# Attention over packed tokens and a Mish layer: both first batches' attention ahead of block 2, a fixed order on all engines up to block 15, and a d_ff order that alternates between batches 0 and 1

## Chip, core and metric

The kernel runs on 1 core of one Trainium2 chip. The metric is device time in microseconds (us) of one execution; lower is better. Float32 arithmetic is carried out on TensorE (PE) as sums of products of float32r halves, so that one product costs three matmuls.

## Reference

For 8 batches of 8 heads, 576 tokens and head width 64, 32 packed tokens per head attend to all keys, and then all queries attend to the packed result. The outcome, 4608 rows of 512, goes through a layer of width 2048 with the Mish function:

```python
p_packed = sm_attn(p, k, v)               # per head: 32 x 64
out = sm_attn(q, p_packed, p_packed)      # per head: 576 x 64
x = out.transpose(0, 2, 1, 3).reshape(B * S, H * D)
h = x @ w_in                              # 4608 x 2048
g = h * tanh(log1p(exp(min(h, 20))))      # Mish; h itself above 20
return g @ w_out                          # 4608 x 512
```

q, k, v and p are float32. The two weight matrices arrive as float64, and the kernel itself turns their 32-bit words into float32.

## The kernel before

**Attention of a batch** (class `Batch`). Eight heads are handled as two groups g of four. `load` issues the DMAs of k, p, q and v. `start` transposes p. `score(g)` transposes the keys (12 PE transposes, three evacuations, tile `kT`), multiplies with p, takes the maxima and subtracts them (L181); `exps` takes the exponentials on ScalarE (ACT) and their sums on VectorE (DVE, L191). `turn(g)` transposes the queries, `turn_weights` the exponentials, `values` multiplies them with v, `turn_values` transposes the result into `ppT`. `match(g)` multiplies queries with `ppT`, and DVE transposes the scores in 32x32 squares (L240). `weigh` is the second softmax (maxima L248, subtraction L249, Exp L252, sums L254, reciprocal, product L257), a DVE transpose (L262) into `at`, and the split into `aT_hi` (ACT, L263) and `aT_lo` (DVE, L264).

**The layer.** Since the second attention only mixes 32 packed rows per head, `packed_w(b, c)` first multiplies `ppT` with 512 columns (chunk c, four chunks) of w_in (tiles `wi`, matmuls L338) and splits the result into `wp_hi` and `wp_lo` (L349, L350). A *block* is 128 columns f of d_ff for one batch. Its `up` is twelve matmuls of 288 columns (L388), six for each half hf, then Mish on ACT (L391, L393) into `g`; `halves` splits g into `g_hi` (L400) and `g_lo` (L401) on DVE. Its `down` is twelve matmuls of 512 columns (L405 to L407), three for each of four row chunks c, summed over the 16 blocks of a batch in four PSUM accumulators `acc`. The last 64 rows of two batches are done together every four blocks (`split`, `down_rest`).

**Weights.** One conversion takes 128 x 512 weights (0.5 MB of words, tile `w_st`): two ACT passes (L295, L296), then on DVE a clamp (L297), a shift (L298), a sign merge (L299) and the addition of the low word (L302). For w_out a split follows, `wo_hi` on ACT (L312) and `wo_lo` on DVE (L313). There are 32 conversions: 16 of w_in, four for each chunk, and 16 of w_out, one for each f. Converted w_in is written to DRAM and fetched again for later batches (`fetch_wi`).

**What sets the order.** PE runs in the order of the source. The other engines' order is chosen by the scheduler of the tile framework when the program is built, and all DMAs are issued on the queue of SyncE (SP). After the attention of batch 0 the loop over t = 0 to 129 begins: block t (batch t div 16, f = t mod 16) goes up while block t - 2 (`LAG`) goes down. During the blocks of batch b the attention of batch b + 1 is taken in small steps from a generator, three for each block. In the blocks of batch 0, two conversions are called for each block (L517), so that all 32 are called by block 11. The PSUM pools are `ps_acc` (4 buffers), `ps_h` (2, for up) and `ps_a` (2, for attention and `packed_w`).

Of the kernel before, what the change touches and what calls it, by code (L numbers as in the profile page):

```python
# [18 lines left out]
KVB = 7  # L19
W2K = 5  # L20
# [8 lines left out]
def body(  # L29
# [76 lines left out]
    def evacuate(dst, src, n=None):  # L106
        if n is None:
            nc.any.tensor_copy(out=dst, in_=src)
        elif n % 2:
            nc.scalar.copy(out=dst, in_=src)  # L110
        else:
            nc.vector.tensor_copy(out=dst, in_=src)

    def transposed(pool, src, g, dst):
        for i in range(NI):
            ps = psum(pool, [P, 4, R], "ps_kq")
            for h in range(4):
                nc.tensor.transpose(out=ps[:, h, :], in_=of_slot(src, g, h)[:, i, :], identity=ident[:R, :R])  # L118
            evacuate(dst[:, i, :, :], ps, i if pool is ps_acc else None)
            yield  # L120
# [15 lines left out]
    class Batch:  # L136
# [5 lines left out]
        def load(self):  # L142
            b = self.b
            self.k_t = [load_heads(k, b, g, "k_t") for g in range(2)]
            self.p_t = att.tile([P, 2, 2, D], F32, name="p_t", bufs=1)
            p_src = p[b].rearrange("(g h) n d -> (h n) g d", g=2)
            for u in range(2):
                nc.sync.dma_start(out=self.p_t[:, :, u, :], in_=p_src)
            self.q_t = [load_heads(q, b, g, "q_t") for g in range(2)]
            self.v_t = [load_heads(v, b, g, "v_t") for g in range(2)]  # L150

        def start(self, pool):
# [5 lines left out]
            self.a1 = att.tile([P, 2, 2, NI, R], F32, name="a1", tag="a", bufs=1)  # L158
# [27 lines left out]

        def exps(self, gs):
# [3 lines left out]
            nc.vector.reduce_sum(out=self.rs[:, gs], in_=a, axis=AX.X)  # L191
            nc.vector.tensor_scalar(out=self.rs[:, gs], in0=self.rs[:, gs], scalar1=1e-9, scalar2=None, op0=ALU.add)
            nc.vector.reciprocal(out=self.rs[:, gs], in_=self.rs[:, gs])

        def turn_weights(self, g, pool):
            self.a1T[g] = att.tile([R, 2, NI, P], F32, name="a1T")
            for u in range(2):
# [3 lines left out]
                evacuate(self.a1T[g][:, u], ps)  # L201
# [41 lines left out]
        def weigh(self, gs):  # L243
            n = gs.stop - gs.start
            G = n * (S // NP)
            a2 = self.a2[:, gs].rearrange("a h g n -> a (h g) n")
            mx = stat.tile([P, 2 * (S // NP)], F32, name="mx2")[:, :G]
# [4 lines left out]
            nc.scalar.activation(out=a2, in_=a2, func=AF.Exp, scale=scale)  # L252
            sm = stat.tile([P, 2 * (S // NP)], F32, name="sm2")[:, :G]
# [14 lines left out]
        def attention(self):  # L268
# [15 lines left out]
            for g in range(2):  # L284
                yield from self.match(g, ps_a)
            self.weigh(slice(0, 2))

    def from_double(dst, src):


        x = src.rearrange("p (n t) -> p n t", t=2)
        low, high = x[:, :, 0], x[:, :, 1]
        bits = dst.bitcast(I32)
        r = wts.tile([P, dst.shape[1]], I32, name="wround", tag="w2k", bufs=W2K)
        nc.scalar.activation(out=dst, in_=high.bitcast(F32), func=AF.Copy, scale=F64_SCALE)  # L295
        nc.scalar.activation(out=r, in_=low.bitcast(U32), func=AF.Copy, scale=2.0 ** -29)  # L296
        nc.vector.tensor_scalar(out=dst, in0=dst, scalar1=F64_HIGH, scalar2=-F64_HIGH, op0=ALU.min, op1=ALU.max)  # L297
        nc.vector.tensor_scalar(out=bits, in0=bits, scalar1=3, scalar2=None, op0=ALU.logical_shift_left)  # L298
        nc.vector.scalar_tensor_tensor(  # L299
            out=bits, in0=high, scalar=-0x80000000, in1=bits, op0=ALU.bitwise_and, op1=ALU.bitwise_or  # L300
        )
        nc.vector.tensor_tensor(out=bits, in0=bits, in1=r, op=ALU.add)  # L302

    def staged(src):
        st = wts.tile([P, 2 * DO], I32, name="w_st", tag="wstage", bufs=3)
        nc.sync.dma_start(out=st, in_=src)
        return st

    def load_wo(i):
        w = wts.tile([P, DO], F32, name="wo32", tag="w2k", bufs=W2K)  # L310
        from_double(w, staged(w_out_v[:, i, :]))
        nc.scalar.copy(out=wo_hi[i], in_=w)  # L312
        nc.vector.tensor_tensor(out=wo_lo[i], in0=w, in1=wo_hi[i].bitcast(F32), op=ALU.subtract)  # L313
# [3 lines left out]
    def load_wi(c, m):  # L317

        g = m // 2
        if m % 2 == 0:  # L320
            wis[0, c, g] = wts.tile([P, 2, FC], F32, name="wi", tag="w32", bufs=4)
        from_double(wis[0, c, g][:, m % 2], staged(w_in_v[:, m, c * 2 * FC:(c + 1) * 2 * FC]))
        if m % 2:
            nc.sync.dma_start(out=w_in_f32[c][:, g], in_=wis[0, c, g])

    def fetch_wi(b, c):
        for g in range(2):
            wis[b, c, g] = wts.tile([P, 2, FC], F32, name="wi", tag="w32", bufs=4)
# [243 lines left out]
```

## Time and profile before

| what | value |
|---|---|
| median of 3 runs | 822.78 us (821.28 to 823.4) |
| profiled execution | 822.64 us |
| its span, first to last instruction | 820.9 us |
| mean granted PE clock | 0.952 |
| PE busy | 768.2 us (94%) |
| DVE busy | 420.6 us (51%) |
| ACT busy | 336.0 us (41%) |
| DMA | 90.02 MB, mean 110 GB/s |

The span is 1.7 us shorter than the profiled execution's time. In the rows below, times are in microseconds from the span's start. A row of the timeline gives start, duration, engine, source line, operation, output and inputs, shapes and, in brackets, the idle time before it and what ended that. A row of groups gives the count, then busy time and mean nanoseconds of one, then idle time before. A row of a table by stretch gives the stretch, its length, then for PE, PE weight loads, DVE, ACT and GpSimd the busy time and the number of instructions, then the granted PE clock, the DMA share and GB/s.

### The profile page before, as it was taken

The page shows a single profiled execution, that of the slowest core. Times are in us where ns is not written, and L with a number is a line of the kernel's source. Part 1 is how long each engine was busy: PE and PEld are TensorE (multiplying, and loading weights), DVE is VectorE, ACT ScalarE, POOL GpSimd, SP SyncE. Part 2 cuts the span into 40 slices and gives each one's busy share as a digit, 9 for nine tenths or more (in the row PEclk, how much of TensorE's full clock was granted, in tenths as well). Part 3 has the DMA queues.
Part 4 walks back from the last instruction along what each step waited for, and adds up shares of the span by engine and source line. Part 5 has one row for each costly group of instructions (what it writes and reads, how often), then busy time and mean ns, then how long its engine had stood idle before and what let it go on. Part 6 is the DMA issues. An engine that isn't in the chain of part 4 may idle for free.

```text
span 820.9 us, 13745 instructions
## 1 busy us (share of the span) xinstructions
PE 768.2 (94%) x5584; PEld 610.4 (74%) x5584; DVE 420.6 (51%) x812; ACT 336.0 (41%) x766; POOL 0.7 (0%) x6
## 2 busy tenths in 40 slices
PE   6607789999999999999999999999999999999997
PEld 4406667787788787877778787877778787888886
DVE  4799895744373435544373435544373445533332
ACT  3557583435242353235242353335242353332221
POOL 0000000000000000000000000000000000000000
PEclk6557789999999999999999999999999999999999
DMA  9967673144311533144411433144311421131002
GB/s 256 287 226 231 207 243 95 52 139 138 110 52 52 143 95 111 52 138 139 110 52 52 132 107 111 52 137 140 110 52 52 122 67 53 52 103 52 1 1 64
DMA packets 43966, 90.02 MB, mean 110 GB/s; under 512 B 8576, under 2 KB 27008, under 8 KB 43904
## 3 DMA queue, kind: packets, MB, share of 16 engines
q1 hardware_dynamic: 43904, 89.15, 35.8%
q8 instruction: 44, 0.72, 0.4%
q14 instruction: 18, 0.15, 0.1%
HBM read 75.50 MB, written 13.63 MB: 109 GB/s over the span
## 4 chain that ended last, share of the span: by engine, by line
PE 88%; DMA 5%; DVE 4%; issue 1%; ACT 1%; SPq 0%; ACTq 0%
PE ps_h L388 25%; PE acc L405 16%; PE acc L407 14%; PE acc L406 14%; PE ps_kq L118 4%; DMA w_st<-in_moe_w_in_dram 4%; PE ps_w L338 4%; PE ps_s L127 3%; PE ps_rest L405 2%; PE ps_rest L407 2%; PE ps_rest L406 2%; PE ps_pp L209 1%; PE ps_a L200 1%; DMA k_t<-in_k_dram 1%; DMA w_st<-in_moe_w_out_dram 1%
## 5 line engine op out<-in xcount | busy, mean ns | idle before, releaser
L405 PE MATMUL acc<-wo_hi,g_hi 128*128 128x512 f32 x512 | 216.5, 423 | 0.0
L391 ACT ACTIVATE g<-ps_h 128x288 f32<-128x288 f32 (+1 forms) x256 | 98.5, 385 | 286.5 <-PE ps_h L388 250.5
L407 PE MATMUL acc<-wo_hi,g_lo 128*128 128x512 f32 x512 | 203.4, 397 | 0.0
L406 PE MATMUL acc<-wo_lo,g_hi 128*128 128x512 f32 x512 | 203.3, 397 | 0.0
L388 PE MATMUL ps_h<-aT_hi,wp_hi 128*128 128x288 f32 x512 | 159.3, 311 | 21.8 <-ACT aT_hi L263 21.1
L400 DVE CAST g_hi<-g 128x512 fp32r<-128x512 f32 x128 | 54.5, 426 | 239.7 <-ACT g L391 239.7
L388 PE MATMUL ps_h<-aT_lo,wp_hi 128*128 128x288 f32 x512 | 153.2, 299 | 1.9 <-DVE aT_lo L264 1.9
L388 PE MATMUL ps_h<-aT_hi,wp_lo 128*128 128x288 f32 x512 | 153.3, 299 | 0.0
L405 PEld LDWEIGHTS acc<-wo_hi,g_hi 128*128 128x128 f32 x512 | 97.4, 190 | 42.7 <-issue 20.4
L388 PEld LDWEIGHTS ps_h<-aT_hi,wp_hi 128*128 128x128 f32 x512 | 98.1, 192 | 39.6 <-ACT aT_hi L263 23.2
L407 PEld LDWEIGHTS acc<-wo_hi,g_lo 128*128 128x128 f32 x512 | 96.9, 189 | 23.7 <-DVE g_lo L401 0.2
L388 PEld LDWEIGHTS ps_h<-aT_lo,wp_hi 128*128 128x128 f32 x512 | 98.4, 192 | 11.3 <-DVE aT_lo L264 2.5
L406 PEld LDWEIGHTS acc<-wo_lo,g_hi 128*128 128x128 f32 x512 | 97.6, 191 | 8.6
L388 PEld LDWEIGHTS ps_h<-aT_hi,wp_lo 128*128 128x128 f32 x512 | 98.4, 192 | 0.0
L401 DVE TENSOR_TENSOR g_lo<-g,g_hi 128x512 fp32r<-128x512 f32 x128 | 88.2, 689 | 5.9
L350 DVE TENSOR_TENSOR wp_lo<-ps_w,wp_hi 128x512 fp32r<-128x512 f32 x64 | 41.3, 682 | 19.0 <-ACT wp_hi L349 19.0
L349 ACT CAST wp_hi<-ps_w 128x512 fp32r<-128x512 f32 x64 | 34.3, 588 | 32.8 <-PE ps_w L338 32.8
L338 PE MATMUL ps_w<-wi,ppT 64*32 64x512 f32 x512 | 35.7, 615 | 0.0
L118 PE MATMUL ps_kq<-ident,k_t 96*128 96x96 f32 x192 | 27.0, 273 | 9.0 <-issue 4.9
L118 PEld LDWEIGHTS ps_kq<-ident,k_t 96*128 96x128 f32 x192 | 23.1, 158 | 16.4 <-issue 6.4
L118 PE MATMUL ps_kq<-ident,q_t 96*128 96x96 f32 x192 | 26.6, 267 | 6.5 <-issue 2.9
L118 PEld LDWEIGHTS ps_kq<-ident,q_t 96*128 96x128 f32 x192 | 22.6, 154 | 13.1 <-issue 4.6
(81 smaller groups left out, 727.0 us busy)
## 6 DMA issues: line engine op xcount, KB each, us to landing
wi<-w_in_f SPq DMA_DIRECT2D x56, 512.0 KB, 4.5
k_t<-in_k_dram SPq DMA_DIRECT2D x32, 288.0 KB, 3.6
q_t<-in_q_dram SPq DMA_DIRECT2D x32, 288.0 KB, 4.8
v_t<-in_v_dram SPq DMA_DIRECT2D x32, 288.0 KB, 3.6
w_st<-in_moe_w_in_dram SPq DMA_DIRECT2D x16, 512.0 KB, 5.2
w_st<-in_moe_w_out_dram SPq DMA_DIRECT2D x16, 512.0 KB, 4.3
out_dram<-o SPq DMA_DIRECT2D x24, 192.0 KB, 2.5
w_in_f<-wi SPq DMA_DIRECT2D x8, 512.0 KB, 5.0
```

The lines of the kernel that those rows point to most:

```text
L118: nc.tensor.transpose(out=ps[:, h, :], in_=of_slot(src, g, h)[:, i, :], identity=ident[:R, :R])
L127: nc.tensor.matmul(out=ps[u][h * NP:(h + 1) * NP, :], lhsT=packT[u * D:(u + 1) * D, h * NP:(h + 1) * NP], rhs=xT[u * D:(u + 1) * D, :, h, ...
L338: nc.tensor.matmul(out=ps[g][h * NP:(h + 1) * NP, :], lhsT=ppTb[row:row + D, g, h * NP:(h + 1) * NP], rhs=wis[b, c, g][row:row + D, h // 2 ...
L349: nc.scalar.copy(out=hi, in_=ps[g])
L350: nc.vector.tensor_tensor(out=lo, in0=ps[g], in1=hi.bitcast(F32), op=ALU.subtract)
L388: nc.tensor.matmul(out=ps, lhsT=w[:, fs], rhs=a[:, g, cs], start=(n == 0), stop=(n == 5))
L391: nc.scalar.activation(out=self.act[:, hf * HALF:hf * HALF + m], in_=ps[:, :m], func=AF.Mish)
L400: nc.vector.tensor_copy(out=hi, in_=self.act)
L401: nc.vector.tensor_tensor(out=lo, in0=self.act, in1=hi.bitcast(F32), op=ALU.subtract)
L405: nc.tensor.matmul(out=acc, lhsT=hi[:, cs], rhs=wh, start=start, stop=False)
L406: nc.tensor.matmul(out=acc, lhsT=hi[:, cs], rhs=wl, start=False, stop=False)
L407: nc.tensor.matmul(out=acc, lhsT=lo[:, cs], rhs=wh, start=False, stop=stop)
```

## The change

1. **Order.** From the start to block 15 DVE, ACT and SP run in source order, as PE does. Outside that stretch the scheduler places them as before.
2. **Attention of batches 0 and 1 in large pieces.** Both are written out before block 2: whole groups at a time, with blocks 0 and 1 and the conversions 0 to 8 placed by hand among them. For these two batches ACT reads the scores from PSUM, with the negative maximum as bias, and gives the sums itself (`exps_now`); the subtraction pass and the sum pass on DVE go.
3. **Order of the blocks.** `TURNS`: batch 0 with f = 0 to 7, batch 1 with f = 0 to 15, batch 0 with f = 8 to 15; from batch 2 on as before. So the second half of w_out and chunks 2 and 3 of w_in are first needed from block 14 on. Batch 0's four accumulators are put aside after its first eight blocks (tiles `part`) and added at its end. A w_in chunk serves both batches before it is replaced; 48 re-fetches remain of 56.
4. **Conversions** are a generator of two halves each (DVE's part, `join`; then the next one's ACT part, `words`, and the split of this one). Blocks 2 to 7 and 11 take three halves each, block 10 one, the others two.
5. **Smaller edits.** `g_hi` is made on ACT in blocks 0 to 15. `wo_hi` and `wo_lo` share a tile; the second eight of these use buffers that staged early weights. `a1`/`a2` have two buffers, `kvq` eight, `w2k` four, `g` two. `peak` and `weigh` are separate steps, and `sums` comes after the queries are turned. The warm-up matmuls use the identity.

```diff
-    def from_double(dst, src):
...
+    class Weight:
...
+        def words(self):
+            self.dst = self.place()
...
+            nc.scalar.activation(out=self.dst, in_=self.high.bitcast(F32), func=AF.Copy, scale=F64_SCALE)
+            nc.scalar.activation(out=self.r, in_=low.bitcast(U32), func=AF.Copy, scale=2.0 ** -29)
+        def join(self):
...
+            nc.vector.tensor_tensor(out=bits, in0=bits, in1=self.r, op=ALU.add)
...
+    turns = TURNS + [(b, 0, NF) for b in range(2, B)]
+    order = [(b, f, f == a, f == e - 1) for b, a, e in turns for f in range(a, e)]
...
+    def conversion(n):
+        while n < len(weights):
+            weights[n].join()
...
+            yield
+            if n + 1 < len(weights):
+                weights[n + 1].fetch()
+                weights[n + 1].words()
+            weights[n].done()
+            n += 1
+            yield
...
-        first.load()
-        convert(2)
-        first.start(ps_a)
-        together(first.score(0, ps_acc))
-        first.exps(slice(0, 1))
...
+        with tc.manual_schedule(engines={mybir.EngineType.DVE, mybir.EngineType.Activation, mybir.EngineType.SP}):
...
+            for g in range(2):
+                first.peak(slice(g, g + 1))
+            second.start(ps_a)
+            second.turn_keys(0)
+            w[3].join()
+            w[3].done()
+            second.score_now(0)
+            first.weigh(slice(0, 1))
...
+            step(0, (0, 0, 0), 0, nc.scalar.copy)
+            together(second.turn(1, ps_acc))
...
+            step(1, (0, 0, 0), 2, nc.scalar.copy)
+            for g in range(2):
+                together(second.turn_values(g, ps_a))
+            for g in range(2):
+                together(second.match(g, ps_acc))
+            for g in range(2):
+                second.peak(slice(g, g + 1))
+            take(conv, 2)
+            second.weigh(slice(0, 1))
+            take(conv, 2)
+            second.weigh(slice(1, 2))
+            take(conv, 2)
+            for t in range(2, START):
+                step(t, (0, 0, 0), 3 if t < 8 or t == 11 else 1 if t == 10 else 2, nc.scalar.copy)
+        for t in range(START, len(order) + LAG):
+            if t in (16, 26):
+                batches[t // 10 + 1].load()
+            step(t, (1, 1, 1), 2, nc.vector.tensor_copy)
```

**DVE, second softmax of batch 0.** In the kernel before, steps of the softmax (`a_428`) stand between parts of two or three conversions (`wi`, `wo_568`, `wo_614`, `wo_580`):

```order
L257 TENSOR_TENSOR a_428<-a_428,sm_460 128x576
L313 TENSOR_TENSOR wo_lo_110<-wo_568,wo_hi_94 128x512
L299 SCALAR_TENSOR_TENSOR wo_614<-w_st,wo_614 128x512
L302 ISA wo_580<-wo_580,wround 128x1024
L297 TENSOR_SCALAR wi<-wi 128x512
L262 STREAM_TRANSPOSE at<-a_428 128x576
```

In the changed kernel the same softmax (`a_414`, second group) runs without a break:

```order
L309 TENSOR_REDUCE sm_582<-a_414 128x18
L310 TENSOR_SCALAR sm_582<-sm_582 128x18
L311 RECIPROCAL sm_582<-sm_582 128x18
L312 TENSOR_TENSOR a_414<-a_414,sm_582 128x576
L317 STREAM_TRANSPOSE at<-a_414 128x576
L319 TENSOR_TENSOR aT_lo<-at,aT_hi 128x576
```

Each instruction there reads what the one ahead of it wrote, where before an instruction of another chain stood between two such.

**PE, the end of the written-out part.** In the changed kernel the last pieces of batch 1's attention (scores `ps_s` against `ppT`) stand ahead of the first `down` (`acc_871`), and `packed_w` of chunk 1 (`ps_w_924`, whose `wi` are conversions 5 to 8) closes block 2:

```order
L276 MATMUL ps_ppT<-ident,pp 128x128 x2
L129 MATMUL ps_s_788<-qT,ppT 32x288 x4
L129 MATMUL ps_s_789<-qT,ppT 32x288 x4
L129 MATMUL ps_s_801<-qT,ppT 32x288 x4
L129 MATMUL ps_s_802<-qT,ppT 32x288 x4
L496 MATMUL acc_871<-wo_91,g_hi 128x512
```

Before, batch 1's attention begins in block 2 and one piece of it stands between two pieces of a block:

```order
L162 MATMUL ps_p<-ident,p_t 128x128 x2
L405 MATMUL acc_679<-wo_hi_93,g_hi 128x512
L406 MATMUL acc_679<-wo_lo_109,g_hi 128x512
L407 MATMUL acc_679<-wo_hi_93,g_lo 128x512
L405 MATMUL acc_680<-wo_hi_93,g_hi 128x512
L406 MATMUL acc_680<-wo_lo_109,g_hi 128x512
L407 MATMUL acc_680<-wo_hi_93,g_lo 128x512
L118 MATMUL ps_kq<-ident,k_t 128x96 x4
```

What moved is all of batch 1's attention, from among blocks 2 to 14 to ahead of block 2.

**DVE, blocks 3 and 4 of the changed kernel.** Conversions (`wo_954`, `wo_979`) and their splits (L412, here of `wo_93`, `wo_94`) take turns with `g_lo`:

```order
L412 TENSOR_TENSOR wo_93<-wo_907,wo_93 128x512
L383 TENSOR_SCALAR wo_954<-wo_954 128x512
L386 TENSOR_SCALAR wo_954<-wo_954 128x512
L387 SCALAR_TENSOR_TENSOR wo_954<-w_st,wo_954 128x512
L390 ISA wo_954<-wo_954,wround 128x1024
L412 TENSOR_TENSOR wo_94<-wo_954,wo_94 128x512
L492 TENSOR_TENSOR g_lo<-g,g_hi 128x512
```

The split of a conversion stands directly behind its last step, so that it waits for the ACT copy in between.

More of the change, by code (lines that the diff above doesn't have):

```diff
@@ new lines, in take, with step @@
+    def take(it, n):
+        for _ in range(n):
+            next(it, None)
+    def step(t, n_att, n_conv, cast):
+        nonlocal gen
+        grp = None
+        if t < len(order):
+            b, f, begin, end = order[t]
+            if t == 20:
+                gen = batches[2].attention()
+            if b > 1 and f == 0 and b + 1 < B:
+                gen = batches[b + 1].attention()
+            if b > 1 and f == 10 and b + 2 < B:
+                batches[b + 2].load()
+            grp = Group(b, f, begin, end, wps[b, f // 4], g_rests[b // 2])
+            grp.tiles()
+        groups.append(grp)
+        dn = groups[t - LAG] if t >= LAG else None
+        if dn:
+            down(dn, 0)
+        if grp:
+            grp.up(0)
+        take(conv, n_conv // 2)
+        take(gen, n_att[0])
+        if dn:
+            down(dn, 1)
+            down(dn, 2)
+        take(gen, n_att[1])
+        if grp:
+            grp.up(1)
+        take(conv, n_conv - n_conv // 2)
+        if grp:
+            grp.halves(cast)
+        if t - 1 in paired:
+            pb, i = paired[t - 1]
+            rest["g"] = split(g_rests[pb // 2][0, i], g_rests[pb // 2][1, i])
+        if dn:
+            down(dn, 3)
+        n = t // 4 + 1
+        if t % 4 == 2 and n < len(chunks):
+            nb, nch = chunks[n]
+            if nch == 0:
+                together(gen)
+            wps[nb, nch] = packed_w(nb, nch)
+            if n >= 7 and n + 1 < len(chunks):
+                fetch_wi(chunks[n + 1][1])
+        else:
+            take(gen, n_att[2])
+        if t - 2 in paired:
+            down_rest(*paired[t - 2])
@@ L487, in body @@
-        together(first.turn_weights(0, ps_acc))
-        together(first.turn(1, ps_a))
-        together(first.turn_weights(1, ps_acc))
-        together(first.values(0, ps_acc), first.values(1, ps_acc))
-        together(first.turn_values(0, ps_a), first.turn_values(1, ps_a))
-        together(first.match(0, ps_acc), first.match(1, ps_acc))
-        for g in range(2):
-            first.weigh(slice(g, g + 1))
-        wps = {(0, 0): packed_w(0, 0)}
-        convert(5)
-        batches[1].load()
```

369 lines of the change are left out of this document (230 added, 139 removed).

## Prediction

> **What bounds the kernel now.** I read first the table by stretch, then who waits, then the chain of waits.
>
> ```profile
> core 0: us, PE busy (x) PEld busy (x) DVE busy (x) ACT busy (x) POOL busy (x), PEclk, DMA share, GB/s
> 0.00:130.00 130.00, 82.01 (x568) 62.63 (x569) 107.15 (x233) 78.05 (x148) 0.70 (x6) 0.70 0.78 234
> 130.00:800.00 670.00, 669.81 (x4939) 534.31 (x4939) 308.54 (x572) 254.56 (x609) 0.00 (x0) 1.00 0.28 87
> ```
>
> From 130 on PE works 669.81 of 670 us at full clock, and the change takes no matmul away: there is nothing to gain there. In the first 130 us PE is busy 82.01 at a mean clock of 0.70, while DVE is busy 107.15. So the question is one number: when does the changed kernel stand where this one stands at 130? Where it stands:
>
> ```profile
> 0.00:130.00 130.00, 23.97 (x108) 20.53 (x108) 0.70 0.78 234
> 0.00:130.00 130.00, 13.77 (x27) 6.42 (x28) 0.70 0.78 234
> 130.94 0.33 PE ps_a L200 x3
> 132.75 0.81 PE ps_pp L209 x48
> 135.16 0.81 PE ps_pp L209 x48
> 140.78 0.65 PE ps_s L127 x16
> 145.82 1.07 PE ps_s L127 x16
> ```
>
> The first row is line 388 alone (108 of its matmuls with PE and PE weight loads), the second line 405: 108 / 12 = 9 blocks are up, and 27 / 4, nearly 7, are down. The other five are the last pieces of batch 1's attention in the chain of waits; they come after 130 and are 3.7 us of PE. All 32 conversions are behind it.
>
> What one block costs PE at full clock is the distance of successive starts:
>
> ```profile
> 302.87 0.29 PE L388 MATMUL ps_h<-aT_hi,wp_hi 128*128 128x288 f32 x1
> 303.00 0.29 PE L388 MATMUL ps_h<-aT_lo,wp_hi 128*128 128x288 f32 x1
> 304.22 0.39 PE L406 MATMUL acc<-wo_lo,g_hi 128*128 128x512 f32 x1
> 304.45 0.39 PE L407 MATMUL acc<-wo_hi,g_lo 128*128 128x512 f32 x1
> ```
>
> 0.13 and 0.23 us, so a block takes 12 x 0.13 + 12 x 0.233 = 4.4 us, and 8.8 at half clock.
>
> **The changed start, stage by stage.** DVE is the engine that all stages lean on, now in source order. Its prices:
>
> ```profile
> L297 DVE TENSOR_SCALAR wi<-wi 128x512 f32<-128x512 f32 x16 | 6.8, 423 | 7.4 <-ACT wi L295 7.3
> L298 DVE TENSOR_SCALAR wi<-wi 128x512 int32<-128x512 int32 x16 | 6.6, 418 | 0.0
> L299 DVE SCALAR_TENSOR_TENSOR wi<-w_st,wi 128x512 int32<-128x512 int32 x16 | 10.8, 683 | 0.0
> L302 DVE CUSTOM_DVE_ANT_0 wi<-wi,wround 128x1024 uint16<-128x1024 uint16 x16 | 10.8, 679 | 0.0
> L248 DVE TENSOR_REDUCE mx<-a 128x18 f32<-128x576 f32 x2 | 1.5, 742 | 0.0
> L249 DVE TENSOR_TENSOR a<-a,mx 128x576 f32<-128x576 f32 x2 | 1.5, 734 | 0.0
> L262 DVE STREAM_TRANSPOSE at<-a 128x576 f32<-128x576 f32 x16 | 12.4, 773 | 0.2
> L264 DVE TENSOR_TENSOR aT_lo<-at,aT_hi 128x576 fp32r<-128x576 f32 x16 | 12.0, 749 | 1.9 <-ACT aT_hi L263 1.9
> 56.97 0.68 DVE L313 TENSOR_TENSOR wo_lo<-wo,wo_hi 128x512 fp32r<-128x512 f32 x1
> 57.57 0.68 DVE L299 SCALAR_TENSOR_TENSOR wo<-w_st,wo 128x512 int32<-128x512 int32 x1
> 803.35 0.43 DVE L400 CAST g_hi<-g 128x512 fp32r<-128x512 f32 x1 [3.05 <-ACT g L391]
> 803.81 0.69 DVE L401 TENSOR_TENSOR g_lo<-g,g_hi 128x512 fp32r<-128x512 f32 x1
> ```
>
> Two instructions that do not depend on each other start 0.60 us apart though one takes 0.68 (at 56.97): 0.08 lies over. Where the second needs the first it starts 0.46 after a 0.43 (at 803.35): 0.03 is added. A conversion's four steps depend on each other, so written in sequence they take 2.2 + 0.1 - 0.08 = 2.2 us, against 1.9 when others stand between; this is the price of source order, 0.3 for each. One group of `weigh` is 0.74 + 0.43 (two small ones) + 0.75 + 0.77 and, after the ACT copy of 0.68, 0.75: 4.3 us with the hand-offs. `peak` for two groups is 2 x (0.74 + 0.73) = 2.9. PE in the early stages and ACT:
>
> ```profile
> 8.81 2.13 PE L118 MATMUL ps_kq<-ident,k_t 96*128 96x96 f32 x12
> 11.68 1.22 PE L127 MATMUL ps_s<-kT,pT 64*32 64x288 f32 x16 [0.74 <-DVE kT L112]
> 36.04 1.96 PE L338 MATMUL ps_w<-wi,ppT 64*32 64x512 f32 x16
> L391 ACT ACTIVATE g<-ps_h 128x288 f32<-128x288 f32 x128 | 52.8, 413 | 135.3 <-PE ps_h L388 99.5 <-issue 22.3 <-ACT wp_hi L349 13.4
> L296 ACT ACTIVATE wround<-w_st 128x512 int32<-128x512 uint32 x32 | 21.3, 669 | 0.0
> L312 ACT CAST wo_hi<-wo 128x512 fp32r<-128x512 f32 x16 | 9.9, 621 | 3.1 <-DVE wo L302 3.1
> ```
>
> *Stage 1, to the last `aT_lo` of batch 0.* p goes ahead of two key loads (2 x 288 KB, 2.5 us at the 234 GB/s of the first row), so the chain starts at about 6 where the first transpose started at 8.4. Link by link: transposes and last copy to 9.2; scores 1.2, maxima 1.0; Exp (two of 0.41, the nearest row) and key copies to 13.4; scores and maxima of group 1 to 16, with one conversion between; ACT words and Exp to 18; copies, a conversion and sums to 20; the second group's queries, values, weight transposes and values again at some 1.5 each (between the first two rows) and a copy of 0.6 to 26.6; `ppT` to 28.4; scores to 30.3; transpose 0.5 and `peak` 2.9: 33.7. Then batch 1's copies 1.2, conversion 3 2.2, maxima 1.2, `weigh` 4.3: 42.6; copy 0.5, a wait of 2.5 for Exp and `packed_w` (1.96), `wp_lo` 1.3: 46.9; maxima 1.2, `weigh` 4.3: **52.4**. Before, the two groups stood at 54 and 62 (below): this is the gain of not letting conversions between.
>
> ```profile
> 53.49 0.61 PE L388 MATMUL ps_h<-aT_hi,wp_hi 128*128 128x288 f32 x1 [15.50 <-ACT aT_hi L263]
> 61.96 0.61 PE L388 MATMUL ps_h<-aT_hi,wp_hi 128*128 128x288 f32 x1 [5.61 <-ACT aT_hi L263]
> ```
>
> *Stage 2, batch 1's attention with blocks 0 and 1.* Copies 2.3, to 54.7, while block 0 goes up at half clock (12 x 0.26, from 54), then Mish and `g_hi` 1.2: DVE waits to 58.3. `g_lo`, copy, sums 1.7; conversion 4 with its wait 2.5; small ones 1.5; a wait of 0.8 for the values, `pp` 0.3; conversion 5 2.2: 67.3. Here ACT has block 1's Mish and the next words (2 x 0.57) ahead of `g_hi`: a wait of 2.8. `g_lo`, `ppT`, scores 1.8, four transposes 1.9, `peak` 2.9: 76.7. Conversion 6, `weigh`, conversion 7, `weigh`, conversion 8: 2.2 + 4.3 + 2.2 + 4.3 + 2.2: **91.9**. PE has finished block 2 by 80 and stands before `packed_w` of chunk 1, which reads conversion 8.
>
> *Stage 3, blocks 2 to 7.* DVE: nine conversions 20.0, seven w_out splits at 0.6 4.2, five of them directly behind their conversion, so that DVE waits for the ACT copy (0.62): 3.3, six `g_lo` 3.7, four `wp_lo` 2.4, in all 33.6, or 5.6 for a block. PE needs 4.4 and with two `packed_w` 28: DVE bounds, and `g_lo` of block 7 is done at **125.5**. ACT has 1.0 of Mish, 0.6 of `g_hi` and some 2.8 of conversions for a block, less than 5.6.
>
> Not in these links: some 30 hand-offs that I rounded off, 0.05 each from the 0.03 above: 1.5. Sums given by Exp on ACT are in no row; between nothing and half a pass of 0.41 each, four on the chain: 0.8, which I take. So 127.8. At that point PE has 9 blocks up, 7 down and both attentions done.
>
> *Moved without cost.* On SP the k and q of batch 2 (8 x 288 KB) now stand ahead of the staging loads from conversion 13 on, and wait for the values of batch 1 at 65; conversion 13 is due at about 110, so 45 us cover some 10 of transfer at the rate above. Were that cover gone, each conversion would wait for its landing,
>
> ```profile
> w_st<-in_moe_w_in_dram SPq DMA_DIRECT2D x16, 512.0 KB, 5.2
> ```
>
> 5.2 us from the issue, against 3.7 from conversion to conversion in stage 3: 1.5 each. ACT's words of conversion 16 need a `wi` buffer that `packed_w` in block 6 reads last; DVE waits there less than 0.7. From block 8 on a block asks of DVE a conversion, 0.6, 0.6 and 0.3, at most 3.7, and in 16 to 19 4.2 with `g_hi`, under 4.4, so PE stays full. One more change of accumulators (eight for seven) puts a copy of 0.7 in front: 1.0 with the final additions.
>
> **Sum.** Against the profiled execution: 820.9 - (130 - 127.8) - 3.7 (attention already done) - 0.7 (the missing quarter block) + 1.0 = 815.3; its time lies 1.7 above its span, so **817.0 us**, 0.7% below 822.64 and 822.78, the median. The changed kernel converts only 18 weights by then where this one has 32; a good part of that relief goes back into the waits of DVE named above.
>
> **Rivals.** *Fast:* in stages 1 and 2 I let PE run at half clock. On the chain lie some dozen PE links of 1.2 to 2.9; at full clock they save about 0.7 each, 8 us: 809. For it: nothing there needs the half clock. Against it:
>
> ```profile
> 10.00:20.00 10.00, 7.04 (x58) 4.26 (x56) 7.85 (x19) 5.39 (x10) 0.00 (x0) 0.50 1.08 303
> ```
>
> the same kind of work, PE 7.04 of 10 busy, got 0.50.
>
> *No change:* stage 3 gives the rest back, by conversions that wait for words or for each other, 0.6 for each of nine: 822.
>
> *Slower:* PE itself falls to half clock in blocks 3 to 7. Then a block is 8.8 against DVE's 5.6, 3.2 lost for each; over four of the five, 13: 830. [...]
>
> ```profile
> 102.00:105.00 3.00, 2.80 (x27) 1.56 (x25) 3.00 (x8) 2.09 (x5) 0.00 (x0) 1.00 0.99 328
> 104.80 2.90 issue
> 105.00:108.00 3.00, 0.30 (x2) 0.34 (x3) 3.00 (x9) 2.80 (x4) 0.00 (x0) 0.81 1.06 288
> 108.00:112.00 4.00, 4.00 (x18) 3.60 (x17) 3.69 (x6) 3.88 (x7) 0.00 (x0) 0.50 0.87 302
> ```
>
> A gap of 2.90 us from full clock was followed by 0.50 though PE was then busy throughout. [...]
>
> **Chances and range.** Forecast, 812 to 820: 0.38. Fast, below 812: 0.20. No change, 820 to 825: 0.18. Slower, above: 0.24. About 0.3% (2.5 us) is what a measurement of this kernel can tell from no change: faster 0.58, same 0.18, slower 0.24. The range runs from 806, with most of the fast case and the sums on ACT free, to 829, the slower case nearly in full.
>
> **What would show it.** Batch 0's second softmax done near 52, where the first `up` of block 0 starts; `packed_w` of chunk 1 near 92 after a PE gap of about 12 us; block 9 near 128 after blocks of 5.6; from there PE full at clock 1.00. Wrong would be: PE at 0.5 in blocks 3 to 7, a wait of ACT for a `w_st` landing there, or gaps of PE after block 9, above all in blocks 16 to 24, where conversions and batch 2's attention meet.

## The result, and the profile after

The changed kernel takes **810.94 us** (median of 4 runs, 809.08 to 812.55) against 822.25 for the kernel before on the same chip: ratio 0.9861 (0.9835 to 0.9887). The same kernel in a second series (e9 below) took 812.90 against 822.24, ratio 0.9887 (0.9860 to 0.9913). So the change saves 9 to 11 us; the forecast was 817.0, which is 5 to 6 saved. The profiled execution took 809.08, the fastest of its four, with a span of 807.3.

The table by stretch of the changed kernel, the same two stretches as before (columns: stretch, length, busy time of PE, PE weight loads, DVE, ACT and GpSimd with their instructions, granted PE clock, DMA share, GB/s):

```profile
0.00:130.00 130.00, 93.43 (x740) 68.62 (x740) 95.63 (x197) 67.44 (x145) 0.70 (x6) 0.80 0.62 182
130.00:800.00 670.00, 669.27 (x4834) 537.89 (x4834) 344.85 (x648) 255.71 (x609) 0.00 (x0) 1.00 0.29 91
```

PE has 11.4 us more behind it at 130 (93.43 against 82.01) and DVE 11.5 less (95.63 against 107.15). After 130 PE is full at clock 1.00 in both, and DVE has 36 us more to do there (344.85 against 308.54), the postponed conversions among it. The clock of the first row, 0.80, is too high: this profile has no clock record ahead of 17.0, and the rows count that time as full clock (1.00 from 0 to 17). The sixteen matmuls of the first scores took 1.22 us there, as long as in the kernel before, where the granted clock was 0.50 (at 11.68, in the prediction's rows), against 0.72 in the profile of e9, whose record has full clock at that point:

```profile
8.90 1.22 PE L129 MATMUL ps_s<-kT,pT 64*32 64x288 f32 x16 [0.57 <-ACT kT L112]
```

```profile
7.94 0.72 PE L129 MATMUL ps_s<-kT,pT 64*32 64x288 f32 x16 [0.57 <-ACT kT L112]
```

The points that the prediction named, as rows of the timeline (start, duration, engine, line, operation, idle time before):

```profile
49.26 0.76 DVE L319 TENSOR_TENSOR aT_lo<-at,aT_hi 128x576 fp32r<-128x576 f32 x1 [0.74 <-ACT aT_hi L318]
...
74.21 1.04 PE L428 MATMUL ps_w<-wi,ppT 64*32 64x512 f32 x2
80.76 1.93 PE L428 MATMUL ps_w<-wi,ppT 64*32 64x512 f32 x8 [5.51 <-DVE wi L390]
...
84.23 0.76 DVE L319 TENSOR_TENSOR aT_lo<-at,aT_hi 128x576 fp32r<-128x576 f32 x1 [0.74 <-ACT aT_hi L318]
...
87.29 1.93 PE L428 MATMUL ps_w<-wi,ppT 64*32 64x512 f32 x6 [4.60 <-DVE wi L390]
90.29 0.79 PE L496 MATMUL acc<-wo,g_hi 128*128 128x512 f32 x1 [1.08 <-ACT wo L411]
...
123.97 0.29 PE L479 MATMUL ps_h<-aT_hi,wp_hi 128*128 128x288 f32 x1
```

Batch 0's last `aT_lo` ends at 50.0 (forecast 52.4), batch 1's at 85.0. `packed_w` of chunk 1 begins at 74.21 and stands still for 5.51 and 4.60 until conversions 7 and 8 are joined; with the wait for `wo` PE idles 11.2 us between 75 and 91. At 123.97 the tenth block starts up, nine are up and seven down, with a quarter of the next: the forecast had that at 127.8.

### The profile page after: what moved, and what is told of

Same layout as the page of the kernel before. It is cut to its first block, busy times and chain, and to the rows that moved or that the text cites. A ratio compares the mean times of both kernels' runs of the same rounds, so it can differ in the third digit from the quotient of the medians.

```text
span 807.3 us, 13715 instructions
## 1 busy us (share of the span) xinstructions
PE 765.5 (95%) x5584; PEld 608.5 (75%) x5584; DVE 441.9 (55%) x846; ACT 323.2 (40%) x752; POOL 0.7 (0%) x6
## 4 chain that ended last, share of the span: by engine, by line
PE 88%; DVE 9%; ACT 2%; issue 1%; DMA 0%; SPq 0%; DVEq 0%; ACTq 0%
PE ps_h L479 25%; PE acc L496 15%; PE acc L498 14%; PE acc L497 14%; PE ps_w L428 4%; PE ps_kq L120 4%; PE ps_s L129 3%; PE ps_rest L496 2%; PE ps_rest L498 2%; PE ps_rest L497 2%; PE ps_pp L260 1%; PE ps_a L251 1%; DVE wi L387 1%; DVE wo L387 1%; DVE wo L390 1%
## 5 line engine op out<-in xcount | busy, mean ns | idle before, releaser
L496 PE MATMUL acc<-wo,g_hi 128*128 128x512 f32 x512 | 214.4, 419 | 1.9 <-ACT wo L411 1.1
L498 PE MATMUL acc<-wo,g_lo 128*128 128x512 f32 x512 | 202.6, 396 | 1.9 <-DVE g_lo L492 1.9
L497 PE MATMUL acc<-wo,g_hi 128*128 128x512 f32 x512 | 202.5, 395 | 0.0
L479 PE MATMUL ps_h<-aT_hi,wp_hi 128*128 128x288 f32 x512 | 157.6, 308 | 0.0
L491 DVE CAST g_hi<-g 128x512 fp32r<-128x512 f32 x112 | 47.8, 426 | 196.6 <-ACT g L482 196.6
L496 PEld LDWEIGHTS acc<-wo,g_hi 128*128 128x128 f32 x512 | 96.7, 189 | 45.1 <-issue 23.9
L498 PEld LDWEIGHTS acc<-wo,g_lo 128*128 128x128 f32 x512 | 96.8, 189 | 25.4 <-DVE g_lo L492 3.1
L497 PEld LDWEIGHTS acc<-wo,g_hi 128*128 128x128 f32 x512 | 97.2, 190 | 8.6 <-DVE wo L412 0.4
L492 DVE TENSOR_TENSOR g_lo<-g,g_hi 128x512 fp32r<-128x512 f32 x128 | 88.2, 689 | 18.0 <-ACT g_hi L491 12.4
L428 PE MATMUL ps_w<-wi,ppT 64*32 64x512 f32 x512 | 40.0, 628 | 13.7 <-DVE wi L390 10.1
L484 ACT ACTIVATE g_rest<-ps_h 128x64 f32<-128x64 f32 x128 | 28.1, 219 | 0.0
L428 PEld LDWEIGHTS ps_w<-wi,ppT 64*32 64x32 f32 x512 | 6.4, 106 | 28.2 <-DVE wi L390 12.7
```

Source lines behind the costliest of these rows:

```text
L428: nc.tensor.matmul(out=ps[g][h * NP:(h + 1) * NP, :], lhsT=ppTb[row:row + D, g, h * NP:(h + 1) * NP], rhs=wis[c, g][row:row + D, h // 2, : ...
L479: nc.tensor.matmul(out=ps, lhsT=w[:, fs], rhs=a[:, g, cs], start=(n == 0), stop=(n == 5))
L484: nc.scalar.activation(out=self.g_rest[self.b % 2, self.f // 4][:, self.f % 4, :], in_=ps[:, m:], func=AF.Mish)
L491: cast(out=hi, in_=self.act)
L492: nc.vector.tensor_tensor(out=lo, in0=self.act, in1=hi.bitcast(F32), op=ALU.subtract)
L496: nc.tensor.matmul(out=acc, lhsT=hi[:, cs], rhs=wh, start=start, stop=False)
```

## The experiments

Times are medians; each ratio is against runs of the kernel before on the same chip (the changed kernel has 0.9861 and 0.9887). "In order" means that an engine runs in source order up to block 15.

| run | edit of the changed kernel | us | ratio (95%) |
|---|---|---|---|
| e1 | old order over d_ff | 842.33 | 1.0249 (1.0234 to 1.0265) |
| e2, e5 | DVE, ACT, SP all left to the scheduler | 801.41, 800.83 | 0.9765 (0.9736 to 0.9794), 0.9731 (0.9714 to 0.9749) |
| e3 | first softmax as before | 814.33 | 0.9909 (0.9896 to 0.9922) |
| e4 | PE's gaps filled | 807.59 | 0.9835 (0.9819 to 0.9851) |
| e6 | SP alone in order | 810.11 | 0.9847 (0.9826 to 0.9869) |
| e7 | w_out split one step later | 813.69 | 0.9889 (0.9872 to 0.9906) |
| e8 | g_hi on DVE | 812.70 | 0.9874 (0.9853 to 0.9896) |
| e9 | none | 812.90 | 0.9887 (0.9860 to 0.9913) |
| e10 | DVE and ACT in order, SP free | 817.84 | 0.9948 (0.9929 to 0.9966) |
| e11, e13 | place of wo_hi and wo_lo | 812.02, 812.67 | 0.9878, 0.9888 |
| e12 | SP in order, 12 weights staged early | 801.59 | 0.9750 (0.9730 to 0.9769) |
| e14 | the same, 8 early | 803.41 | 0.9774 (0.9760 to 0.9787) |
| e15 | the same, 6 early | 808.71 | 0.9843 (0.9822 to 0.9863) |
| e16 | e12 with PE's gaps filled | 802.38 | 0.9755 (0.9741 to 0.9768) |
| e17 | kernel before, without the warm-up's tile of zeros: tiles 512 bytes lower | 830.93 | 1.0116 (1.0098 to 1.0134) |
| e18 | e12 with w_out splits on GpSimd | 807.53 | 0.9822 (0.9809 to 0.9836) |

### Where the gain comes from: the order over d_ff

```diff
-TURNS = [(0, 0, 8), (1, 0, 16), (0, 8, 16)]
+TURNS = [(0, 0, 16), (1, 0, 16)]
...
-step(t, (0, 0, 0), 3 if t < 8 or t == 11 else 1 if t == 10 else 2, nc.scalar.copy)
+step(t, (0, 0, 0), 4 if t < 14 else 2, nc.scalar.copy)
```

> The changed kernel with the old order over d_ff (batch 0 with f = 0 to 15, then batch 1), the conversions put into the order in which they are then needed, two for each block up to block 13; everything else as changed. Theory A (the postponed conversions carry the gain): after conversion 8, at 87.2 us in the changed kernel, DVE still has 23 conversions at 2.2, 15 w_out splits at 0.6 with about as much waiting, 12 g_lo and 8 wp_lo at 0.6 ahead of block 15: 81 us, so to 168, where PE needs 12 blocks of 4.4 and three packed_w, 56. PE is then short of work by up to 25 us, of which blocks that are already up give back some 8: 822 to 830. Theory B (the written-out attention of two batches carries it): 811 to 815.

It took 842.33, 20 us more than the kernel before, 29 to 31 more than the changed one and 12 above the upper end of theory A. Its table by stretch over blocks 3 to 13, and what PE waited for from 95 to 190 (us in total, times, longest):

```profile
97.00:176.00 79.00, 61.53 (x283) 48.18 (x283) 60.45 (x108) 45.43 (x98) 0.00 (x0) 0.85 0.42 141
```

```profile
PE acc L496 <- ACT g_hi L491: 11.2, 5, 2.8
PE acc L496 <- ACT wo L411: 8.8, 3, 4.0
```

PE is busy 61.53 of 79 and waits 20 us for halves of g and of w_out. So, with the engines in source order, the postponed conversions carry the whole gain, and source order with long pieces of attention, without them, is a loss. Here the prediction's slower rival shows too: waits of up to 4.0 us, and a mean granted clock of 0.85 over these blocks, where the changed kernel has 1.00 from 95.5 on. What the old order over d_ff would cost with the engines left to the scheduler was not run.

### Source order is not a gain but a price

```diff
-with tc.manual_schedule(engines={mybir.EngineType.DVE, mybir.EngineType.Activation, mybir.EngineType.SP}):
+with tc.manual_schedule(engines={mybir.EngineType.PE}):
```

> The changed kernel with DVE, ACT and SP left to the scheduler from the start; PE's order and all instructions as changed. Theory A (source order carries a part: the softmax of batch 0 runs unbroken): conversions come between its steps again, stage 1 ends at 55 to 60 instead of 50.0 and the whole is 815 to 821. Theory B (source order costs 0.3 for each conversion and 0.6 for each split, as the prediction priced it, and the scheduler spares that): 806 to 809. No matter: 810 to 812.

> The same kernel as in the run with the scheduler free, for a profile of an execution near its median: there the profiled execution was the slowest of six (809.0 against a median of 801.4) and began with a wait of 6.8 us of PE for keys. Theory A (a late landing at the start alone made it slow): the profile is at 799 to 803, PE full from 77 to 80, as far ahead of 84 as the landing was late. Theory B (the clock decides): the keys land late again, but the stretches at 0.5 between 9 and 84 are shorter.

Neither theory of e2 went far enough: 801.41, 9.5 less than the changed kernel (11.5 less than e9). Its profiled execution was its slowest (809.02); e5 profiled one of 799.88 and went by theory A, with PE's clock at 1.00 from 77.2 on. Two more runs split the three engines:

```diff
+with tc.manual_schedule(engines={mybir.EngineType.SP}):                                        # e6
+with tc.manual_schedule(engines={mybir.EngineType.DVE, mybir.EngineType.Activation}):          # e10
```

> The changed kernel with SP alone in source order up to block 15, and DVE and ACT left to the scheduler. Theory A (DVE's and ACT's source order is what costs the changed kernel 9.5 us): 799 to 804, and steadier than the free one since keys, queries and values go ahead of staged weights. Theory B (the order of the DMAs is what the free one gains by): 809 to 812.

> The changed kernel with DVE and ACT in source order up to block 15 and SP left to the scheduler (the fourth of the four combinations: all in order 810.9, none 801, SP alone in order 810.1). Theory A (the order of the DMAs alone costs 9): 800 to 803. Theory B (weights that are staged early only help where DVE may take them up early, and in source order conversions 4 to 8 stand where they stand): 808 to 811, less only what ACT waits for landings now.

With SP alone in order the time is that of the changed kernel (810.11, theory B). With SP alone free it is worse than either, 817.84: outside both expectations. There staged weights go ahead of batch 0's second half of values and of batch 1's keys, DVE may not use them yet, and PE waits for those values and keys (us in total, times, longest, up to 60):

```profile
PE ps_kq L120 <- DMA k_t<-in_k_dram: 5.8, 2, 4.6
PE ps_pp L260 <- DMA v_t<-in_v_dram: 4.9, 2, 4.2
```

Each half alone brings nothing; together they bring 9.5. The reason shows in e12, where SP stays in order and only the loads of staged weights move:

```diff
-for g in range(2):
-    first.load_v(g)
 w[2].fetch()
 w[3].fetch()
+first.load_v(0)
+for n in range(4, 8):
+    w[n].fetch()
+first.load_v(1)
+for n in range(8, 12):
+    w[n].fetch()
...
-w[4].fetch()
...
-w[5].fetch()
...
-for n in range(6, 11):
-    w[n].fetch()
```

> The run with SP alone in order, with one difference: the loads of staged weights 2 to 11 are written among and directly behind batch 0's values, ahead of batch 1's keys, instead of among batch 1's loads. DVE and ACT are left to the scheduler. Theory A (what the free scheduler gains by is that weights are there while DVE has nothing else to do in the first 70 us): 800 to 803, 15 or 16 conversions joined by 72, PE full at 1.00 from 77 to 82. Theory B (something else in the scheduler's DMA order): 806 to 810.

801.59: theory A. Its timeline: conversion 8, the last `aT_lo` of batch 0, `packed_w` of chunk 1, and the last `aT_lo` of batch 1; then its table by stretch.

```profile
37.74 0.64 DVE L390 CUSTOM_DVE_ANT_0 wi<-wi,wround 128x1024 uint16<-128x1024 uint16 x1
...
60.48 0.76 DVE L319 TENSOR_TENSOR aT_lo<-at,aT_hi 128x576 fp32r<-128x576 f32 x1
...
83.44 1.09 PE L428 MATMUL ps_w<-wi,ppT 64*32 64x512 f32 x16
...
92.32 0.75 DVE L319 TENSOR_TENSOR aT_lo<-at,aT_hi 128x576 fp32r<-128x576 f32 x1
```

```profile
0.00:72.00 72.00, 41.24 (x414) 28.87 (x418) 58.43 (x144) 43.49 (x89) 0.70 (x6) 0.64 0.92 284
...
80.00:128.00 48.00, 47.53 (x287) 38.23 (x285) 30.90 (x57) 28.95 (x65) 0.00 (x0) 1.00 0.24 77
```

Conversion 8 is joined at 38.4 instead of 87.2, so `packed_w` of chunk 1 runs through without a wait, and from 80 on PE is full at 1.00. Batch 1's attention ends *later* than in the changed kernel (93.1 against 85.0), and that costs nothing, because batch 1 first goes up in block 8. What PE needs first is chunk 1 for block 4. The source order of the changed kernel has these two the wrong way round: conversions 6 to 8 stand behind batch 1's `peak` and between its two `weigh`.

How much of it can be had was tried with fewer early loads:

> The run with early staging, with the loads of weights 8 to 11 put back behind batch 1's loads: eight weights early instead of twelve. Theory A (DVE is full from 15 to 72 in the run with early staging, and conversions 9 to 15, 2.8 us each with their split, are done there ahead of need): four of them move behind 70, where DVE is busy 15 of 20 us, and batch 1's attention is done up to 10 us sooner: 793 to 799. Theory B (each conversion kept out of the start comes back in blocks 3 to 8, where DVE bounds): 801 to 806.

> As before, but only weights 0 to 5 early; 6 and 7 behind batch 1's queries, 8 to 11 behind its values. Theory A: as good as or better than eight early, 793 to 799. Theory B: between eight early and none (810.1): 803 to 808.

803.41 and 808.71, theory B for both (e15 above its upper end by 0.7): fewer is worse. The same stretch in e14, in e15, in the changed kernel and in e10:

```profile
0.00:72.00 72.00, 45.35 (x472) 32.48 (x472) 54.80 (x135) 39.50 (x83) 0.70 (x6) 0.65 0.96 291
```

```profile
0.00:72.00 72.00, 40.53 (x360) 28.27 (x361) 49.41 (x124) 34.20 (x71) 0.70 (x6) 0.60 0.89 272
```

```profile
0.00:72.00 72.00, 48.47 (x517) 35.99 (x518) 47.26 (x112) 31.97 (x70) 0.70 (x6) 0.76 0.87 247
```

```profile
0.00:72.00 72.00, 47.27 (x468) 33.94 (x469) 40.92 (x99) 27.98 (x62) 0.70 (x6) 0.81 0.91 252
```

DVE's busy time up to 72 nearly orders the executions: 58.43 (e12, span 798.9), 54.80 (801.0), 49.41 (807.7), 47.26 (807.3), 40.92 (817.1); the profiles of e5 (59.15, 798.1), e6 (45.57, 808.9) and e9 (44.30, 810.7) fall in line, that of e2 (52.88, 807.2) less so. From e10 to e12 that is 18.2 us for 17.5 of DVE work done early, about one for one. PE's busy time in the same stretch orders nothing (41.24 in the best, 48.47 in the changed kernel). The clock of the last two rows is no measure, since their profiles have no clock record ahead of 17.0 and 33.8. One caution: e12, e14 and e15 are scheduled anew, and e17 shows what that alone can do; the trend is the evidence, not one pair, and it is a trend, not a separate experiment on DVE.

### PE's clock at the start

```diff
+def fill(n):
+    ps = ps_h.tile([P, P], F32, name="ps_fill", tag="ps_h")
+    for _ in range(n):
+        nc.tensor.matmul(out=ps, lhsT=ident, rhs=ident, start=True, stop=True)
...
+fill(10)
 wps = {(0, 0): packed_w(0, 0)}
```

> The changed kernel with 71 more matmuls of the identity (of no use, written over PSUM that is free) in the places where PE waits longest between 12 and 87 us, so that PE is hardly idle. Theory A (in stages 1 and 2 the PE links set the pace, and which stretches are granted full clock decides 2 to 3 us in each stage): the clock is 1.00 from about 30 on; packed_w of 2.4, scores of 1.8, the two first blocks up of 2.8 and the first matmuls after 87 halve, 1.3 + 0.9 + 1.3 + 1.2 + 2.5, about 7 us less: 803 to 806. Theory B (DVE alone sets the pace there): 810 to 812, or 812 to 814 where a filling overruns its gap. Theory C (the filling doesn't raise the clock): the clock rows stay at 0.5 as before and the time is 811 to 815.

> The run with early staging and the matmuls of the identity of the filled run (44 of them, without those inside packed_w of chunk 1). Theory A (with DVE full, PE's clock no longer matters: executions of the free kernel at a mean clock of 0.995 took 802, those at 0.965 took 801): 800 to 803, the clock above 0.98. Theory B (PE's links are still on the chain): 797 to 799, as much less as the filling brought to the changed kernel.

The filling raised the clock of the first 92 us: 0.87 in e4, by its table, where the changed kernel has 0.66 in e9. The profile of the result has 0.74, and about 0.68 (an estimate) if the time from 5.6, where the record of e9 begins, to 17.0 is taken at half clock. The profiled execution of e4 took 810.33, 2.7 above its median.

```profile
0.00:92.00 92.00, 67.09 (x698) 53.31 (x698) 62.65 (x139) 40.90 (x85) 0.70 (x6) 0.87 0.82 217
```

It brought 3 to 5 us in source order, half of what theory A had, and nothing where weights are staged early (802.38 against 801.59). So where DVE is kept busy, a higher clock of PE (a mean of 0.981 to 0.987 in e16's executions, 0.959 to 0.965 in e12's) brought nothing that shows.

### The parts on DVE that the prediction priced

```diff
 weights[n].join()
+if n > 5:
+    weights[n - 1].done()
...
-weights[n].done()
```

> The changed kernel with the split of a conversion written behind the next conversion's last DVE step in place of its own, so that DVE has no wait of 0.69 for the ACT copy in blocks 2 to 7. Theory A (DVE bounds stage 3, as the prediction has it): five or six waits of 0.69 and a part of the PE waits at 107 and 118 (0.6 and 1.3): 2 to 3.5 us, 807.5 to 809. Theory B (PE bounds it, its blocks already up hide the waits): 810 to 812.

> The changed kernel with the first softmax of batches 0 and 1 as before: DVE subtracts the maximum (two of 0.51 for each group) and sums (0.68 for each group), Exp works in place. Theory A (these passes were on the chain of stages 1 and 2): four groups times 1.6, less the 0.8 which the prediction charged for sums on ACT: 5 to 6 us, 816 to 817. Theory B (DVE has slack at these places, PE and ACT are the links there): 810 to 812.

> The changed kernel with g_hi on DVE in blocks 0 to 15, as before. Theory A (DVE bounds up to block 8): 0.43 for each of eight blocks, less the waits for ACT's g_hi that go (0.5 for each of two in stage 2, some 0.6 in block 7): 2 to 3 us, 813 to 814. Theory B (ACT's queue ahead of g_hi cost more than that): 807 to 810.

e7 gained nothing, and lies above both its theories: 0.9889 against 0.9861 and 0.9887. What DVE waited for from 92 to 127, in the unaltered kernel (e9) and in e7:

```profile
DVE wo L412 <- ACT wo L411: 4.2, 6, 0.8
DVE g_lo L492 <- ACT g_hi L491: 0.6, 1, 0.6
```

```profile
DVE wo L383 <- ACT wo L378: 2.3, 2, 2.0
DVE g_lo L492 <- ACT g_hi L491: 1.6, 2, 0.9
DVE wo L412 <- ACT wo L411: 0.4, 1, 0.4
```

Of the six waits for the split one is left, as meant, and DVE stands nearly as long (4.3 against 4.8), mostly for other work of ACT. e3 lost 1.4 to 3.4, between its two theories. e8 can't be told from the changed kernel. In its profile (815.93, the slowest of its four) DVE no longer waits for `g_hi` between 92 and 127, and PE waits 2.8 us for `g_hi` from DVE.

### The same kernel once more, and the rest after the start

> The changed kernel unaltered, on the same chip and beside the next three, since its profiled execution was the fastest of four (809.1 against 810.9) and began with a shorter wait of PE for the second group's keys (1.1 us at 12, against 3.6 at 10 in the kernels that share its start). Theory A (the sums of stages 1 and 2 were nearly right and that execution had a lucky start): conversion 8 is joined at 89 to 92 instead of 87.2, and the rest, from the ninth block up, takes 683 to 684 as there. Theory B (those sums were 4 to 5 us too long): 87 to 88 again. Time 809 to 812 by both.

Theory A, with the median (812.90) 0.9 above its range. In this execution (812.43, close to the median) conversion 8 is joined at 90.5 and the tenth block starts at 127.2:

```profile
89.80 0.69 DVE L390 CUSTOM_DVE_ANT_0 wi<-wi,wround 128x1024 uint16<-128x1024 uint16 x1
```

```profile
127.21 0.29 PE L479 MATMUL ps_h<-aT_hi,wp_hi 128*128 128x288 f32 x1
```

Most of the difference between the two executions arises in a stretch where their clocks differ, first in the profile of the result, then in e9:

```profile
17.00:27.20 10.20, 6.37 (x153) 4.16 (x151) 8.49 (x24) 6.20 (x15) 0.00 (x0) 1.00 1.08 312
```

```profile
17.00:27.20 10.20, 7.67 (x118) 5.75 (x116) 7.35 (x20) 6.32 (x15) 0.00 (x0) 0.50 1.08 312
```

The same kind of work at full and at half clock: 153 matmuls against 118. Conversion 1 is joined at 19.2 and 19.4, conversion 3 at 34.0 and 36.9. Ahead of it the clocks stood the other way round: e9 has full clock from 5.6 to 12.4 and joins conversion 0 at 13.1, the result's execution at 14.5. That lead is lost because ACT, in source order, waits in both for the load of conversion 1, to 16.3 and 16.1, and can't take up attention's next pieces meanwhile.

Past the tenth block both take 683.3 to 683.5 (807.3 - 123.97, 810.7 - 127.21), where the forecast left 687.5 (815.3 - 127.8). Between the first `up` of block 36 and of block 127, where both kernels run the same blocks in the same order with PE full, the kernel before has these rows:

```profile
291.98 0.29 PE L388 MATMUL ps_h<-aT_hi,wp_hi 128*128 128x288 f32 x1
...
804.16 0.29 PE L388 MATMUL ps_h<-aT_hi,wp_hi 128*128 128x288 f32 x1
```

and the changed one these:

```profile
280.57 0.30 PE L479 MATMUL ps_h<-aT_hi,wp_hi 128*128 128x288 f32 x1
...
790.84 0.29 PE L479 MATMUL ps_h<-aT_hi,wp_hi 128*128 128x288 f32 x1
```

512.18 against 510.27: 1.9 us for the same matmuls, 21 ns for a block. The profiles of the changed kernel and its variants have 510.1 to 510.3 there, except e3 with 510.7. By the records it lies in the `down` matmuls alone: from the second to the third of a group it is 0.233 us from start to start before and 0.231 after. Three runs looked for it in the place of the tiles; the edits of two:

```diff
-wo = [const.tile([P, 2, DO], F32R, name=f"wo{i}") for i in range(NF // 2)]
+wo = [[const.tile([P, DO], F32R, name=f"wo_{n}{i}") for n in ("hi", "lo")] for i in range(NF // 2)]                 # e11
+wo = [[const.tile([P, DO], F32R, name=f"wo_{n}{i}") for i in range(NF // 2)] for n in ("hi", "lo")]                 # e13
+wo = list(zip(*wo))                                                                                                 # e13
```

> The changed kernel with wo_hi and wo_lo of the first eight f in tiles of their own again, the second eight as changed. In the kernel before the second matmul of a down takes 0.2331 us to the next start on average, in every run of the changed kernel 0.2311 to 0.2313, which over 1728 matmuls is 3 us that no step of the prediction has. Theory A (the shared tile does it): 0.233 for f under 8 and 0.231 from 8 on, time 1 to 2 us more, 811.5 to 813. Theory B (it is not the layout but where the tiles come to lie, or something else): the pattern over f changes in another way or not at all, time within 1 us.

> The changed kernel with the first eight wo_hi in a row and the first eight wo_lo in a row behind them, 16 KB apart for each f as in the kernel before they lay 32 KB apart; in the run with two tiles they lay where the shared tile lies. Theory A (the place of hi and lo makes a matmul of a down 1.9 ns shorter): f under 8 goes from 0.231 to 0.233, f from 8 on stays; 1.5 us more. Theory B (another cause, so the layout is out): the same pattern over f as before within 0.5 ns, time as the changed kernel.

> The kernel before with one small tile of zeros left out (its warm-up matmuls take the identity, as in the changed kernel), so that all later tiles lie 512 bytes lower, w_out's at the offset within 2 KB that they have in the changed kernel. Theory A (it is the place of the tiles): the second matmul of a down takes 0.231 instead of 0.233 from start to start, time 3 us less, 819 to 820. Theory B (something else of the change): 0.233, 821 to 823; the cause then stays open.

e11 put the tiles at the addresses of the shared one, so it says only that sharing has no cost. e13 moved them 16 KB apart and changed nothing: 0.231. In e17 (in the kernel *before*, the warm-up reads the identity, and its tile of zeros is left out) it stayed at 0.233. Neither the distance of hi and lo nor the 512 bytes are the cause. e3, made for another question, holds both lengths in one program: from block 36 on the blocks with f under 8 have 0.2332, like the kernel before, and those with f from 8 on 0.2314, like the changed one. The first eight tiles of w_out come from one pool and the second eight from another, so this points to where a tile of w_out lies; no run tests what e3 moved, and the cause stays open. e17 told something else: its time went up by 8.6 us. PE has the same order there but for the warm-up, and the scheduler, given one tile less, put the start's instructions on DVE, ACT and SP into another order.

### GpSimd as a helper

```diff
-nc.vector.tensor_tensor(out=lo, in0=self.dst, in1=hi.bitcast(F32), op=ALU.subtract)
+nc.gpsimd.tensor_tensor(out=lo, in0=self.dst, in1=hi.bitcast(F32), op=ALU.subtract)
```

> The run with early staging, with the splits of w_out (wo_lo, 16 of 0.69 on DVE) on GpSimd, which is idle. Theory A (DVE bounds the start): eight splits by 75 us are 5.5 us of DVE; 4 to 5 us less where GpSimd does them in time, 796 to 799. Theory B (DVE's time is filled by what is there, but PE, ACT and hand-offs are the chain): 800 to 803. Theory C (GpSimd is slower and slows DVE while both run): above 803, with longer DVE rows beside its instructions.

Theory C, 807.53. Groups of instructions (count, busy us, mean ns): the split on GpSimd, and steps of w_out's and w_in's conversions on DVE:

```profile
L412 POOL TENSOR_TENSOR wo<-wo,wo 128x512 fp32r<-128x512 f32 x16 | 27.4, 1709 | 146.0 <-ACT wo L411 146.0
```

```profile
L390 DVE CUSTOM_DVE_ANT_0 wo<-wo,wround 128x1024 uint16<-128x1024 uint16 x16 | 13.7, 858 | 0.5
L390 DVE CUSTOM_DVE_ANT_0 wi<-wi,wround 128x1024 uint16<-128x1024 uint16 x16 | 10.8, 679 | 0.1
L386 DVE TENSOR_SCALAR wo<-wo 128x512 int32<-128x512 int32 x16 | 8.6, 540 | 0.2
L386 DVE TENSOR_SCALAR wi<-wi 128x512 int32<-128x512 int32 x16 | 6.6, 418 | 0.1
```

A split that took DVE 0.69 takes GpSimd 1.27 to 1.88; the mean of 1.71 holds one first record of 6.66. The means of w_out's steps on DVE, 858 against 679 ns and 540 against 418, mix untouched instructions with a few that took two to three and a half times as long. One such pair, first GpSimd, then DVE:

```profile
46.08 1.27 POOL L412 TENSOR_TENSOR wo<-wo,wo 128x512 fp32r<-128x512 f32 x1 [1.42 <-ACT wo L411]
```

```profile
46.41 1.23 DVE L383 TENSOR_SCALAR wo<-wo 128x512 f32<-128x512 f32 x1
```

This step takes 0.42 elsewhere; here it began 0.33 into the split and ended 0.29 behind it. What held it up is not shown by these rows. What of the 6 us between e12 and e18 comes from such longer steps, and what from an order made anew, was not separated.

## Why the prediction was right in direction and wrong in size

*What bounds it.* Right that the start decides, and that the question is when PE stands where it stood. Wrong was "the change takes no matmul away: there is nothing to gain there". From the tenth block on the changed kernel needs 4 us less than the sum left: the `down` matmuls are shorter, 21 ns for each of some 120 blocks, 2.5 us, for a cause that stays open; the first quarter of one more block was already down, 0.7; and of the 1.0 charged for the eighth set of accumulators PE shows one wait of 0.6. The last half microsecond I can't place.

*Stages 1 and 2.* In e9 conversion 8 was joined at 90.5, forecast 91.9, and in the profile of the result at 87.2. The sums were nearly right for an execution near the median. The assumption under them, PE at half clock throughout, holds only in part: full clock from 17 to 27 made 2.7 of the 3.3 us by which the first profile is ahead. PE's gap at `packed_w` of chunk 1 was forecast as about 12 and is 11.2 and, in e9, 11.6.

*Stage 3.* From conversion 8 to `g_lo` of block 7 DVE was to need 33.6; it took 36.3 in both executions (123.58 - 87.24, 126.82 - 90.49). Its waits for ACT alone are 4.8 in e9, where the sum has 3.3. What covers the rest in the sum are the 2.3 added at its end, for hand-offs of all stages and for sums on ACT, which belong to stages 1 and 2. So in e9 a start that is 1.4 early, a stage that is 2.7 long and 2.3 added leave a miss of 0.6: that the tenth block came near the forecast is in part luck. The bound was named rightly only in part: e7 removed most of the split's waits and the stage stayed as long, since ACT takes their place.

*So the step that failed* is the sum's last line, "820.9 - (130 - 127.8) - 3.7 - 0.7 + 1.0". It failed above all in what it takes over unchanged: the remainder past the tenth block, put at 687.5, took 683.3 and 683.5, 4 less in both executions. The start, put at 127.8, came at 127.2 in e9 and at 124.0 in the profile of the result. By medians the miss is 4.1 (812.90) to 6.1 (810.94).

*The reasons.* The prediction put stage 1's earlier end down to the gain "of not letting conversions between". The runs say otherwise: with conversions between (e12) batch 0's last `aT_lo` comes 11 us later, at 61.2, and the kernel is 9 to 11 us faster. What brings the gain is that only 18 conversions are needed by then instead of 32, which the prediction named only as relief that partly goes back; e1 puts 29 to 31 us on it. The rest of the change, source order with it, gives back 20 of these (e1 against the kernel before), and 9.5 to 11.5 come back when the three engines are left to the scheduler (e2).

*The rivals.* The fast one (809) came near in time, but not in its cause: a clock of 0.87 instead of 0.66 to 0.68 brought 3 to 5 us, not 8, though 0.87 isn't full clock yet. The row held against it (0.50 at 7.04 busy) does not decide: in the profile of the result the same kind of work, PE 6.37 of 10.2 busy, had 1.00. No change fell with the result. The slower one didn't occur in the changed kernel (1.00 from 95.5 on) and did in e1 (a mean of 0.85 from 97 to 176).

## What to carry to other kernels

Order work by when it is first needed, not by the unit it belongs to: here a weight chunk for block 4 stood behind an attention for block 8, and PE idled 11 us. Work that is to fill an engine's idle time must have its data there: the scheduler could use DVE's spare time only when the loads were issued early, and early loads helped only when the scheduler could use them, so such a pair is to be tried together. The fastest versions here are the changed kernel with DVE, ACT and SP left to the scheduler (801) or with twelve weights staged early (802); and before a scheduled kernel's few microseconds are put down to an edit, one should know what an edit that changes no part of the work does, here 8.6 us.

## What was not expected of the hardware

- The same `down` matmuls run 0.8% faster in the changed kernel, 0.231 against 0.233 us from start to start, 1.9 us of a stretch of 512. In e3 both lengths occur in one program, parted by which eight tiles of w_out are read. The cause isn't found.
- GpSimd, idle otherwise, was not free help in e18: a DVE step of 0.42 us that began 0.33 into a GpSimd split of 1.27 took 1.23 and ended 0.29 after it.
- One program's executions differ in whether PE has full clock in a stretch: from 17.0 to 27.2 it was 1.00 in the profile of the result and 0.50 in e9, and across it the first gained 2.7 us on the second.
